# Two tiles' input products as 2 by 2 blocks with seven block products, in a pooled-attention and gated feed-forward kernel

## Chip, cores and metric

The kernel runs on one core of a Trainium2 chip. The metric is the device time of one execution in microseconds; the median of several runs is compared. A profile of one execution, taken by the hardware profiler, shows what each engine did.

## The reference

```python
# B, H, S, D = 8, 8, 576, 64; d_model 512, d_ff 1536; all float32
k_p = k.reshape(B, H, Sp, 8, D).mean(axis=3)          # Sp = 72
v_p = v.reshape(B, H, Sp, 8, D).mean(axis=3)
scores = scale * np.matmul(q, k_p.transpose(0, 1, 3, 2))
scores = scores - np.max(scores, axis=-1, keepdims=True)
attn = np.exp(scores)
attn = attn / (np.sum(attn, axis=-1, keepdims=True) + 1e-09)
x = np.matmul(attn, v_p)        # then to [4608 tokens, 512]
out = ((x @ w_a) * (x @ w_b)) @ w_out
```

Attention over pooled keys and values gives 4608 rows of 512; a feed-forward part multiplies two projections of them and projects back.

## The kernel before

The 4608 tokens are cut into nine tiles of 512. For each tile and each of twelve feature blocks of 128 (`f`), `ffn_in` computes the two input products (names `a` and `b`) into the PSUM tiles `psa` and `psb`, `gated` multiplies them, and `ffn_out` adds the output product into the four PSUM tiles `acc`. Float32 precision is kept by splitting every operand into a high part of a shorter type and a low part, the difference: each product is three matmuls, high by high, high by low, low by high (lines 618 to 620 and 640 to 642). So a feature block of one tile costs 24 matmuls of 512 columns for the inputs (4 slices of the 512 model dimensions, 3 matmuls, 2 names) and 12 for the output. The high part is a copy on ScalarE (lines 264, 588), the low part a subtraction on VectorE or POOL (`low_part`, line 185).

The weights lie whole in SBUF (`raw`). They arrive as 64-bit words and are turned into float32 by ScalarE and VectorE while tiles 0 and 1 are computed (`convert_weights`). For every tile each weight block is split anew (`split_weight`), on POOL after tile 0.

The attention is computed in chunks of up to 128 queries of one batch (`chunk`): queries split, scores into `psc`, softmax, transposes of the probabilities into `ptr`, and, for blocks of chunks of up to 256 queries in tiles 0 and 1 and up to 384 later, the value products `po`, which are split into the tile's `xh` and `xl`. PSUM tiles of the attention share the tag `att` with two buffers. Keys and values of a batch are pooled by `load_keys` and `load_values`.

The order of all this is written by a small scheduler, `Chains`: every piece of side work is a generator that yields a number of steps; each call of `chains.step()` in the matmul loops (one for six large matmuls) lets those that are due write their next instructions, and one group of small matmuls (`yield PE`). The list `order` holds the large products (tiles 0 and 1 interleaved, because the weights come slowly there; then tile by tile, the output product one block behind), and `plan` the step at which each split, chunk and load begins. All DMAs are issued by SyncE (SP), in the order in which they were written. Every engine works through its own instructions in order.

Of the kernel before, what the change touches and what calls it, by code (L numbers as in the profile page):

```python
# [9 lines left out]
F32 = mybir.dt.float32  # L10
# [39 lines left out]
SLOTS = 6  # L50
TILE_SLOTS = SLOTS * NF

BLOCK, BLOCK_LATER = 256, 384
# [13 lines left out]
IN, OUT = 4, 2  # L67
# [4 lines left out]
CHUNK = 33  # L72
SECOND_GAP, SECOND_START = 1, 14
KEYS_AHEAD, VALUES_AFTER = 18, 14
# [49 lines left out]
def attn_moe_kernel(ctx: ExitStack, tc: tile.TileContext, q, k, v, vr, wa, wb, wo, out):  # L124
# [16 lines left out]
    raw = {name: const.tile([P, NF, 512], F32, name=f"w{name}_raw") for name in ("a", "b", "o")}  # L141
# [8 lines left out]
    work = sb.tile([P, 2 * NK * BLOCK_LATER], I32, tag="work", name="words", bufs=1)  # L150
# [21 lines left out]
    while start < len(flat):  # L172
        stop = start
        while stop < len(flat) and flat[stop][0] == flat[start][0] and tile_of[stop] == tile_of[start]:
            stop += 1
        blocks += cut(list(range(start, stop)), BLOCK if tile_of[start] < 2 else BLOCK_LATER)[1]
# [3 lines left out]
    early_p = {}  # L180
    upcoming = {name: [] for name in ("a", "b", "o", "h")}
    held = dict.fromkeys(upcoming, 0)
# [5 lines left out]
    early_q = raw["a"][:, NF - early:, :].rearrange("p c (g s) -> p c g s", g=NK)  # L188
    early_k = raw["b"].rearrange("p f c -> p (f c)")[:, NF * 512 - NK * S:].rearrange("p (g s) -> p g s", g=NK)
    early_v = raw["o"][:, NF - NK:, :]  # L190
    early_vr = raw["o"][:, NF - NK - NG:NF - NK, :]
# [17 lines left out]
    def convert_weights(name, j, first):  # L209
# [11 lines left out]
        for f in range(NF):  # L221
            words = area[name].rearrange("p (c w) -> p c w", w=2)
            hi, lo = words[:, :, 1], words[:, :, 0]
            w = raw[name][:, f, :]
# [15 lines left out]
            yield 2  # L240

# [16 lines left out]
    def split_weight(name, x):  # L258
        f = x % NF
        yield from wait(("weight", name, f))  # L260
        yield from room(name, x)
        hi = sb.tile([P, 512], F32R, tag=f"jh{name}", name=f"jh{name}_{x}")
        lo = sb.tile([P, 512], F32R, tag=f"jl{name}", name=f"jl{name}_{x}")
        nc.scalar.copy(hi, raw[name][:, f, :])  # L264
        yield 1
        low_part(nc.vector if x < NF and name != "o" else nc.gpsimd, lo, raw[name][:, f, :], hi)
        parts[name, x] = hi, lo

    def load_keys(b):
        kd = kdiag[b % 2]  # L270
        kp = tmp(f"kp_{b}")[:, :NK * SP].rearrange("p (g s) -> p g s", g=NK)
        for g0 in range(0, NK, 2):
# [3 lines left out]
            else:  # L276
# [5 lines left out]
                yield 4  # L282
# [25 lines left out]
            mark("keys", b, g0)  # L308

    def load_values(b):  # L310
        vd = vdiag[b % 2]
        vrem = sb.tile([P, NG, 2, 2, D], F32R, tag="vrem", name=f"vrem_{b}")
        yield from wait(("keys", b, 2), ("values", b - 1))
        vp = sb.tile([P, NK + NG, D], F32, tag="vp", name=f"vp_{b}", bufs=1)
        for x0 in range(0, NK + NG, 2):
            if b == 0:
                vraw = [early_v[:, x, :] if x < NK else early_vr[:, x - NK, :] for x in (x0, x0 + 1)]
            else:
# [8 lines left out]
                yield 3  # L327
# [12 lines left out]
            yield 1  # L340
        for e in range(2):
            r = slice(e * KM, e * KM + KM)
            nc.scalar.mul(vd[r, :, 0, r], vp[r, :NK], 1.0 / POOL)
# [36 lines left out]
    def chunk(i):  # L380
# [5 lines left out]
        else:  # L386
            qraw = tmp(f"qraw_{i}").rearrange("p (g s) -> p g s", g=NK)
            if soon:
                yield from wait(("scores", i - 2))
            load_raw_queries(i, qraw)  # L390
            yield 3 if soon else 5
# [5 lines left out]
        low_part(nc.gpsimd if first else nc.vector, ql[:, :, :n], qraw[:, :, :n], qh[:, :, :n])  # L397
# [17 lines left out]
        if i < SUMMED:  # L415
            for g0 in range(0, NK, 2):
                yield from wait(("keys", b, g0))
                yield PE
                if first:
                    pt = ps.tile([P, 512], F32, tag="acc", name=f"psc_{i}_{g0}", bufs=4)  # L420
                else:
                    pt = ps.tile([P, 512], F32, tag="att", name=f"psc_{i}_{g0}", bufs=2)
                for j in range(2):
                    g = g0 + j
                    for x, (qq, w) in enumerate(((qh, 0), (qh, 1), (ql, 0))):
                        nc.tensor.matmul(
                            pt[:n, j * hk:(j + 1) * hk],
                            qq[:, g, :n],
                            kd[:, g, w].rearrange("p e s -> p (e s)"),
                            start=(x == 0),  # L430
                            stop=(x == 2),
                        )
                less_max(slice(2 * g0, 2 * g0 + 4), pt[:n, :2 * hk].rearrange("p (h s) -> p h s", h=4))
        else:
            for g in range(NK):
                yield from wait(("keys", b, g - g % 2))
                if g % 2 == 0:
                    yield PE
                pt = ps.tile([P, 512], F32, tag="att", name=f"psc_{i}_{g}", bufs=2)
                nc.tensor.matmul(  # L440
                    pt[:n, :2 * hk], qh[:, g, :n], kd[:, g].rearrange("p w e s -> p (w e s)"), start=True, stop=False
                )
                nc.tensor.matmul(  # L443
                    pt[:n, :hk], ql[:, g, :n], kd[:, g, 0].rearrange("p e s -> p (e s)"), start=False, stop=True
                )
                nc.vector.tensor_reduce(
                    out=s[:n, 2 * g:2 * g + 2, :].rearrange("p h s -> p (h s)"),
                    in_=pt[:n, :2 * hk].rearrange("p (w c) -> p c w", w=2),
                    axis=AX.X,
                    op=ALU.add,  # L450
                )
                if g % 2 and g < NK - 1:
                    yield 1
            yield 1
            less_max(slice(0, H), s[:n])
# [36 lines left out]
        def turn(x):  # L492
            rows = P if x < 2 else NR
            num = NK if x < 2 else NG
            if x not in turned[j]:
                if j == 0:

                    if x != 1:
# [303 lines left out]
```

## Time and profile before

| | us |
|---|---|
| median of 3 runs | 1068.54 |
| lowest, highest | 1067.54, 1070.07 |
| profiled execution, first to last instruction (its span; the profile shows nothing outside it) | 1069.4 |
| tiles 0 and 1, from the first large matmul to tile 2 (50.24 to 297.91) | 247.67 |
| tile 4, tile 5, tile 6, tile 7 | 113.0, 110.4, 114.3, 108.6 |

The mean granted TensorE clock of the execution is 0.992 of full speed. The DMA queues moved 63.26 MB, 59 GB/s in the mean. In the profile's tables, PE is TensorE, PEld its weight loads, DVE is VectorE, ACT ScalarE, POOL GpSimd, SPq SyncE's queue. A matmul's length in the timeline is that of its pipeline; how fast matmuls follow each other is read from their starts. "idle before, releaser" is the time for which an engine had nothing to do just before a group's instructions, and what ended it.

### The profile page before, as it was taken

To read this page: it belongs to the slowest core of one execution; us is meant where nothing else is said; L and a number is where in the kernel's file an instruction comes from. 1 tells how busy PE (TensorE), PEld (TensorE's weight loads), DVE (VectorE), ACT (ScalarE), POOL (GpSimd) and SP (SyncE) were. 2 spreads that over 40 slices of the span, in tenths; PEclk is the share of its full clock that TensorE was granted. 3 is DMA by queue.
4 is the path that set the end of the run, shared out by engine and by line. 5 is a ranking of instruction groups with operands and counts; after the bars stand their busy time and mean duration, and the time that the engine had idled before them with its cause. 6 is when DMAs were issued, how large, how long until landed. Compare 5 with 4: busy or idle time off the path is not lost.

```text
span 1069.4 us, 13397 instructions
## 1 busy us (share of the span) xinstructions
PE 1029.1 (96%) x4964; PEld 855.9 (80%) x4964; DVE 622.7 (58%) x941; ACT 515.1 (48%) x1037; POOL 520.8 (49%) x427
## 2 busy tenths in 40 slices
PE   4678999999999999999999999999999999999998
PEld 4556788888878888888887888888887888888886
DVE  7997967955674455644676456654668444423222
ACT  3756745554553445544544454444545444443332
POOL 6331200255474555555556555555556455554443
PEclk9988999999999999999999999999999999999999
DMA  6343445330330003100320002100220010001001
GB/s 218 117 137 119 138 125 193 116 131 2 105 111 1 1 23 110 46 1 1 97 91 1 1 28 84 45 1 1 94 71 14 1 60 1 1 1 40 1 1 40
DMA packets 31889, 63.26 MB, mean 59 GB/s; under 512 B 7344, under 2 KB 7344, under 8 KB 31824
## 3 DMA queue, kind: packets, MB, share of 16 engines
q1 hardware_dynamic: 31824, 62.40, 18.3%
q8 instruction: 39, 0.64, 0.2%
q14 instruction: 26, 0.21, 0.1%
HBM read 51.12 MB, written 11.27 MB: 58 GB/s over the span
## 4 chain that ended last, share of the span: by engine, by line
PE 88%; DVE 7%; ACT 3%; issue 1%; DMA 0%; POOL 0%; SPq 0%; DVEq 0%; ACTq 0%; POOLq 0%
PE acc L640 9%; PE psa L618 9%; PE acc L642 9%; PE psb L618 9%; PE acc L641 9%; PE psa L620 9%; PE psa L619 9%; PE psb L620 9%; PE psb L619 9%; PE ptr L521 2%; PE psc L440 2%; PE po L558 1%; PE po L559 1%; PE psc L443 1%; PE po L557 1%; PE po L556 1%
## 5 line engine op out<-in xcount | busy, mean ns | idle before, releaser
L185 POOL TENSOR_TENSOR jlo<-wo_raw,jho 128x512 fp32r<-128x512 f32 x108 | 141.2, 1308 | 423.5 <-ACT jho L264 423.4
L625 ACT COPY h<-psa 128x512 f32<-128x512 f32 x108 | 63.5, 588 | 255.6 <-PE psa L620 234.0
L575 DVE TENSOR_TENSOR h<-psb,h 128x512 f32<-128x512 f32 x108 | 74.1, 686 | 191.9 <-PE psb L620 186.2
L640 PE MATMUL acc<-jho,hh 128*128 128x512 f32 x432 | 173.6, 402 | 0.0
L618 PE MATMUL psa<-xh,jha 128*128 128x512 f32 x432 | 173.2, 401 | 0.4 <-DVE xl L185 0.4
L618 PE MATMUL psb<-xh,jhb 128*128 128x512 f32 x432 | 171.2, 396 | 0.0
L619 PE MATMUL psa<-xl,jha 128*128 128x512 f32 x432 | 169.9, 393 | 0.1
L620 PE MATMUL psa<-xh,jla 128*128 128x512 f32 x432 | 169.9, 393 | 0.0
L642 PE MATMUL acc<-jho,hl 128*128 128x512 f32 x432 | 169.4, 392 | 0.0
L641 PE MATMUL acc<-jlo,hh 128*128 128x512 f32 x432 | 169.2, 392 | 0.0
L620 PE MATMUL psb<-xh,jlb 128*128 128x512 f32 x432 | 168.4, 390 | 0.0
L619 PE MATMUL psb<-xl,jhb 128*128 128x512 f32 x432 | 168.2, 389 | 0.0
L185 POOL TENSOR_TENSOR jla<-wa_raw,jha 128x512 fp32r<-128x512 f32 x89 | 134.4, 1510 | 8.5 <-ACT jha L264 8.5
L185 DVE TENSOR_TENSOR hl<-h,hh 128x512 fp32r<-128x512 f32 x101 | 106.6, 1055 | 28.8 <-ACT hh L588 28.1
L185 POOL TENSOR_TENSOR jlb<-wb_raw,jhb 128x512 fp32r<-128x512 f32 x89 | 118.0, 1326 | 0.1
L620 PEld LDWEIGHTS psa<-xh,jla 128*128 128x128 f32 x432 | 82.0, 190 | 17.7
L642 PEld LDWEIGHTS acc<-jho,hl 128*128 128x128 f32 x432 | 81.5, 189 | 17.6
L620 PEld LDWEIGHTS psb<-xh,jlb 128*128 128x128 f32 x432 | 81.1, 188 | 17.2
L618 PEld LDWEIGHTS psa<-xh,jha 128*128 128x128 f32 x432 | 81.9, 190 | 16.0 <-DVE xl L185 0.7
L619 PEld LDWEIGHTS psa<-xl,jha 128*128 128x128 f32 x432 | 82.1, 190 | 15.7 <-DVE xl L185 0.5
L185 DVE TENSOR_TENSOR ql<-qraw,qh 128x512 fp32r<-128x512 f32 (+1 forms) x36 | 41.6, 1157 | 90.0 <-ACT qh L395 90.0
L618 PEld LDWEIGHTS psb<-xh,jhb 128*128 128x128 f32 x432 | 81.1, 188 | 15.4 <-DVE h L575 0.2
(102 smaller groups left out, 1737.6 us busy)
## 6 DMA issues: line engine op xcount, KB each, us to landing
out<-y SPq DMA_DIRECT2D x36, 256.0 KB, 2.0
kraw<-in_k SPq DMA_DIRECT2D x28, 288.0 KB, 3.2
vraw<-in_v SPq DMA_DIRECT2D x28, 256.0 KB, 3.0
qraw<-in_q SPq DMA_DIRECT2D x28, 256.0 KB, 3.6
words<-in_wa SPq DMA_DIRECT2D x12, 512.0 KB, 3.6
words<-in_wb SPq DMA_DIRECT2D x12, 512.0 KB, 3.7
words<-in_wo SPq DMA_DIRECT2D x12, 512.0 KB, 3.6
vraw<-in_vr SPq DMA_DIRECT2D x14, 192.0 KB, 2.5
```

Of the source, the lines that this page charges most:

```text
L185: eng.tensor_tensor(out=lo, in0=src, in1=hi.bitcast(F32), op=ALU.subtract)
L440: nc.tensor.matmul(pt[:n, :2 * hk], qh[:, g, :n], kd[:, g].rearrange("p w e s -> p (w e s)"), start=True, stop=False)
L443: nc.tensor.matmul(pt[:n, :hk], ql[:, g, :n], kd[:, g, 0].rearrange("p e s -> p (e s)"), start=False, stop=True)
L521: nc.tensor.transpose(ptr[:rows, g, :n], src, ident[:n, :n])
L575: nc.vector.tensor_tensor(out=h, in0=pt, in1=h, op=ALU.mult)
L618: nc.tensor.matmul(pt, wh[:, c], xh[:, kk], start=(kk == 0), stop=False)
L619: nc.tensor.matmul(pt, wh[:, c], xl[:, kk], start=False, stop=False)
L620: nc.tensor.matmul(pt, wl[:, c], xh[:, kk], start=False, stop=(kk == NK - 1))
L625: nc.scalar.copy(h, pt)
L640: nc.tensor.matmul(acc[c], hh[:, cs], wh, start=first, stop=False)
L641: nc.tensor.matmul(acc[c], hh[:, cs], wl, start=False, stop=False)
L642: nc.tensor.matmul(acc[c], hl[:, cs], wh, start=False, stop=last)
```

## The change

Tiles 0 and 1 stay as they were, but for the attention around them. Tile 2 is computed alone, all input products first, then all output products. Tiles 3 to 8 are taken in pairs. For a pair and a feature block, the two tiles are the rows, the two halves of the model dimensions the inner index and the names a and b the columns of a 2 by 2 block product. Its eight block products are replaced by seven, of weight sums and differences (`T1` to `T4`, `A0`, `A1`, `B1`) with sums of the tiles' halves (`X00`, `X01`, `X11`, `S1` to `S4`), and additions of the results. `both` does this: 7 x 2 x 3 = 42 large matmuls, five additions on VectorE that read PSUM, two operations on POOL and two copies on ScalarE. Three PSUM banks hold the products: `psa`, `psb`, and one of the two of the tag `att`. The first tile's output product runs in the gaps of the next blocks; the second's gated values go to DRAM (`keep_later`) and come back for twelve output blocks in a row after the pair.

- The weight sums are made once, on POOL, ScalarE and VectorE, while tiles 1 and 2 run (`sums_of_weights`), and written to DRAM with the split parts of `a` and `b` (`jd`); the converted output weights go there too (`od`). In the pairs SBUF holds four buffers of 2 MB, and `loads` streams one feature block's fourteen parts and its output weights into each.
- The attention's results of tiles 2 to 8 go to DRAM unsplit (`xd`). `whole_x` loads tile 2's; `sums_of_x` loads a pair's and makes and splits the seven sums, at the output products that stand before the pair.
- The attention of tiles 2 to 4 is planned beside tiles 0 to 2, that of tiles 5 and 6 beside the first pair, of 7 and 8 beside the second. From the tenth chunk on, scores are six matmuls of 144 columns for half a chunk and copied by ScalarE, where two of 288 and two of 144 were added up by VectorE. Value blocks are at most 256 queries. The low parts of later queries move from VectorE to POOL.

The core of the diff (the new `sums_of_weights`, `loads` and `sums_of_x` are told above):

```diff
-BLOCK, BLOCK_LATER = 256, 384
+BLOCK = 256
-IN, OUT = 4, 2
+IN, OUT, BOTH, REST = 4, 2, 9, 3
+PAIRS = [(3, 4), (5, 6), (7, 8)]
...
-        low_part(nc.vector if x < NF and name != "o" else nc.gpsimd, lo, raw[name][:, f, :], hi)
+        shared = name == "o" and (t in (1, 2) or t > 3 and t % 2 == 0 and f % 2)
+        low_part(nc.vector if x < NF and name != "o" or shared else nc.gpsimd, lo, src, hi)
...
+                to = big(f"j{at}_{f}")
+                nc.sync.dma_start(to[:, :2 * JW], jd[f].rearrange("p h c s -> p (h c s)"))
+                nc.sync.dma_start(to[:, 2 * JW:], od[:, f])
...
+            if i < SUMMED:
+                less_max(slice(2 * g0, 2 * g0 + 4), src)
+            else:
+                nc.scalar.copy(s[:n, 2 * g0:2 * g0 + 4], src)
...
+    def both(p, f):
+        t0, t1 = PAIRS[p]
+        need(lambda: (p, f) in stream and ("combos", p, S4) in done)
+        w, xs = stream[p, f], combos[p]
+        u, v, r = banks if f % 2 == 0 else (banks[2], banks[1], banks[0])
...
+        product(u, A0, X00)
+        nc.scalar.copy(first, u)
+        product(v, T2, S2)
+        add(nc.vector, first, v, first)
+        rest(0)
+        product(u, A1, X01, start=False)
+        product(r, T3, S3)
+        add(nc.vector, third, r, first)
+        chains.step()
+        rest(1)
+        product(v, T1, S1)
+        nc.scalar.copy(fifth, v)
+        product(r, T4, X11)
+        add(nc.gpsimd, fifth, fifth, third)
+        add(nc.vector, fourth, r, third)
+        add(nc.gpsimd, fifth, fifth, fourth, ALU.mult)
+        rest(2)
+        product(v, B1, S4, start=False)
+        add(nc.vector, first, v, first)
+        add(nc.vector, first, u, first, ALU.mult)
...
-    for t in range(2, NTILE):
-        for f in range(NF):
-            order.append(("in", t, f))
-            if f:
-                order.append(("out", t, f - 1, f == 1, False))
+    order += [("in", 2, f) for f in range(NF)] + [("out", 2, f, f == 0, f == NF - 1) for f in range(NF)]
+    for p, (t0, t1) in enumerate(PAIRS):
+        order += [("both", p, f) for f in range(NF)] + [("rest", p)]
+        order += [("out", t1, f, f == 0, f == NF - 1) for f in range(NF)]
```

Two places show how the order of instructions changes. First TensorE, before, inside a feature block of tile 3 (`psc` are scores, `psa` an input product, each row one matmul):

```order
L440 MATMUL psc_0_4313<-kdiag_75,qh_4236 128x288
L443 MATMUL psc_0_4313<-kdiag_75,ql_4237 128x144
L440 MATMUL psc_1_4317<-kdiag_75,qh_4236 128x288
L443 MATMUL psc_1_4317<-kdiag_75,ql_4237 128x144
L618 MATMUL psa_5_4301<-xh_3125,jha_4246 128x512
L619 MATMUL psa_5_4301<-xl_3126,jha_4246 128x512
L620 MATMUL psa_5_4301<-xh_3125,jla_4247 128x512
```

And TensorE after, inside the third block of the first pair (`bank` are the seven products, six matmuls each, `acc` output products of earlier blocks, a quarter at a time):

```order
L820 MATMUL bank_psa<-x_1_4059,j_2_4371 128x512 x6
L820 MATMUL bank_att<-x_5_4060,j_2_4371 128x512 x6
L885 MATMUL acc_3_4688<-jo_later,hh_4493 128x512
L886 MATMUL acc_3_4688<-jo_later,hh_4493 128x512
L887 MATMUL acc_3_4688<-jo_later,hl_4494 128x512
L618 MATMUL psc_0_4695<-kdiag_78,qh_4616 64x144 x2
L618 MATMUL psc_0_4695<-kdiag_78,ql_4617 64x144
L618 MATMUL psc_0_4695<-kdiag_78,qh_4616 64x144 x2
L618 MATMUL psc_0_4695<-kdiag_78,ql_4617 64x144
L820 MATMUL bank_psb<-x_3_4061,j_2_4371 128x512 x6
```

The quarters of an output product and the attention's groups now stand between products of six, and half a chunk's scores are six matmuls of 144 columns.

Second VectorE, before, at the ninth to eleventh feature block of tile 2 (`h` is the gate, `hl` its low part, `kp` and `kdiag` the keys of a later batch, `ql` and `xl` low parts of queries and attention results):

```order
L185 TENSOR_TENSOR hl_3574<-h_3529,hh_3573 128x512
L575 TENSOR_TENSOR h_3606<-psb_9_3608,h_3606 128x512
L185 TENSOR_TENSOR hl_3655<-h_3606,hh_3654 128x512
L284 TENSOR_REDUCE kp_3626<-kraw_0_3627 128x72
L284 TENSOR_REDUCE kp_3626<-kraw_1_3628 128x72
L185 TENSOR_TENSOR ql_3696<-qraw_3624,qh_3695 128x512
L575 TENSOR_TENSOR h_3689<-psb_10_3691,h_3689 128x512
```

And VectorE after, at four output blocks of tile 2 (`back` are gated values from DRAM, `jo_later` the output weights' parts, `temp` and `x` the sums for the first pair and their low parts):

```order
L216 TENSOR_TENSOR hl_4096<-back_4037,hh_4095 128x512
L216 TENSOR_TENSOR jo_later<-wo_0_3500,jo_later 128x512
L402 TENSOR_TENSOR temp_4127<-x_3987 128x512 x2
L216 TENSOR_TENSOR hl_4116<-back_4069,hh_4115 128x512
L216 TENSOR_TENSOR jo_later<-wo_0_3500,jo_later 128x512
L402 TENSOR_TENSOR temp_4128<-temp_4127,x_3987 128x512 x2
L216 TENSOR_TENSOR hl_4144<-back_4099,hh_4143 128x512
L216 TENSOR_TENSOR jo_later<-wo_0_3500,jo_later 128x512
L472 TENSOR_REDUCE kp_3925<-kraw_2_4085 128x72
L216 TENSOR_TENSOR hl_4169<-back_4119,hh_4168 128x512
L216 TENSOR_TENSOR x_4_4058<-temp_4128,x_4_4058 128x512 x2
L216 TENSOR_TENSOR jo_later<-wo_0_3500,jo_later 128x512
```

Where a block of 36 large matmuls had a gate and a low part, an output block of 12 now has a low part of the gate, one of the weights, and two operations of the pair's sums between them. The row that follows is the second reduction of `kp`.

More of the change, by code (lines that the diff above doesn't have):

```diff
@@ L175, in attn_moe_kernel @@
             stop += 1
-        blocks += cut(list(range(start, stop)), BLOCK if tile_of[start] < 2 else BLOCK_LATER)[1]
+        blocks += cut(list(range(start, stop)), BLOCK)[1]
         start = stop
@@ L258, in split_weight @@
     def split_weight(name, x):
-        f = x % NF
-        yield from wait(("weight", name, f))
-        yield from room(name, x)
-        hi = sb.tile([P, 512], F32R, tag=f"jh{name}", name=f"jh{name}_{x}")
-        lo = sb.tile([P, 512], F32R, tag=f"jl{name}", name=f"jl{name}_{x}")
-        nc.scalar.copy(hi, raw[name][:, f, :])
+        t, f = divmod(x, NF)
+        if t < 3 and (name != "o" or t < 2):
+            yield from wait(("weight", name, f))
+            src = raw(name, f)
+        else:
+            while name == "o" and x not in wo_later:
+                yield 1
+            src = wo_later[x]
@@ L269, in load_keys, with claim, of_batch @@
+    busy = set()
+    def claim(what):
+        while what in busy:
+            yield 1
+        busy.add(what)
+    def of_batch(b):
+        return [i for i in range(len(flat)) if flat[i][0] == b]
     def load_keys(b):
+        yield from wait(*(("scores", i) for i in of_batch(b - 2)))
+        if b:
+            yield from claim("kv")
         kd = kdiag[b % 2]
@@ L387, in chunk @@
             qraw = tmp(f"qraw_{i}").rearrange("p (g s) -> p g s", g=NK)
-            if soon:
-                yield from wait(("scores", i - 2))
+            yield from wait(("scores", i - 2))
             load_raw_queries(i, qraw)
-            yield 3 if soon else 5
+            yield 3 if soon else 8
         yield from wait(("scores", i - 2))
@@ L413, in less_max @@
             )
[L415 to L453, printed above, removed]
@@ new lines, in chunk @@
+        for g0 in range(0, NK, 2):
+            yield from wait(("keys", b, g0))
+            yield PE
+            if first:
+                pt = ps.tile([P, 512], F32, tag="acc", name=f"psc_{i}_{g0}", bufs=4)
+            else:
+                pt = ps.tile([P, 512], F32, tag="att", name=f"psc_{i}_{g0}", bufs=2)
+            for j in range(2):
+                g = g0 + j
+                for x, (qq, w) in enumerate(((qh, 0), (qh, 1), (ql, 0))):
+                    nc.tensor.matmul(
+                        pt[:n, j * hk:(j + 1) * hk],
+                        qq[:, g, :n],
+                        kd[:, g, w].rearrange("p e s -> p (e s)"),
+                        start=(x == 0),
+                        stop=(x == 2),
+                    )
+            src = pt[:n, :2 * hk].rearrange("p (h s) -> p h s", h=4)
+            if i < SUMMED:
+                less_max(slice(2 * g0, 2 * g0 + 4), src)
+            else:
+                nc.scalar.copy(s[:n, 2 * g0:2 * g0 + 4], src)
+                yield 1
@@ L628, in attn_moe_kernel, with keep_later, rest_of, ffn_out @@
+    def keep_later(x, h):
+        later[x] = dram.tile([P, NT], F32, name=f"later_{x}")
+        nc.sync.dma_start(later[x], h)
+        yield 1
+    waiting = []
+    def rest_of(p):
+        while waiting:
+            if len(waiting) % 2 == 0:
+                chains.step()
+            waiting.pop(0)()
     acc = {}
-    def ffn_out(t, f, first, last):
+    def ffn_out(t, f, first, last, cs=None):
         x = t * NF + f
@@ L633, in ffn_out @@
         (wh, wl), (hh, hl) = parts["o", x], parts["h", x]
-        for c in range(NT // P):
-            if c % 2 == 0:
+        for c in cs or range(NT // P):
+            if c % 2 == 0 and not cs:
                 chains.step()
```

337 lines of the change are left out of this document (271 added, 66 removed).

## The prediction

> **What bounds the kernel now.** I read the page first, then a table of windows cut at the stages, then the order of time on TensorE.
>
> ```profile
> span 1069.4 us, 13397 instructions
> PE 1029.1 (96%) x4964; PEld 855.9 (80%) x4964; DVE 622.7 (58%) x941; ACT 515.1 (48%) x1037; POOL 520.8 (49%) x427
> PE   4678999999999999999999999999999999999998
> PE 88%; DVE 7%; ACT 3%; issue 1%; DMA 0%; POOL 0%; SPq 0%; DVEq 0%; ACTq 0%; POOLq 0%
> ```
>
> TensorE is busy for 96% of the span and carries 88% of the chain that ends last; VectorE's 7% lies at the start. The stages show it (windows; the columns are named in the first line):
>
> ```profile
> core 0: us, PE busy (x) PEld busy (x) DVE busy (x) ACT busy (x) POOL busy (x), PEclk, DMA share, GB/s
> 0.00:50.24 50.24, 27.69 (x145) 25.27 (x145) 42.43 (x81) 26.08 (x58) 24.57 (x34) 1.00 0.54 175
> 50.24:99.66 49.42, 39.80 (x183) 30.94 (x183) 42.01 (x71) 30.67 (x65) 12.81 (x12) 0.83 0.39 120
> 99.66:123.42 23.76, 20.63 (x107) 16.07 (x105) 22.25 (x38) 15.76 (x33) 8.67 (x7) 1.00 0.44 133
> 123.42:209.15 85.73, 85.45 (x386) 70.36 (x386) 67.52 (x110) 46.17 (x86) 8.10 (x6) 1.00 0.48 152
> 209.15:229.22 20.07, 20.07 (x108) 17.05 (x106) 13.14 (x21) 9.41 (x20) 10.47 (x8) 1.00 0.13 47
> 229.22:250.18 20.96, 20.96 (x103) 17.51 (x102) 13.06 (x21) 10.45 (x22) 10.80 (x9) 1.00 0.39 129
> 250.18:297.91 47.73, 47.73 (x233) 40.16 (x232) 28.19 (x43) 24.29 (x51) 26.43 (x22) 1.00 0.20 63
> 297.91:408.50 110.59, 110.15 (x544) 91.39 (x542) 63.00 (x98) 53.77 (x114) 63.46 (x51) 1.00 0.13 39
> 855.79:964.36 108.57, 108.57 (x529) 90.97 (x528) 45.34 (x62) 49.10 (x96) 60.47 (x48) 1.00 0.05 15
> 964.36:1065.20 100.84, 100.80 (x445) 83.17 (x443) 25.46 (x28) 34.53 (x62) 43.01 (x34) 1.00 0.04 13
> 1065.20:1069.40 4.20, 0.00 (x0) 0.00 (x0) 0.69 (x1) 0.00 (x0) 0.00 (x0) 0.96 0.54 199
> ```
>
> Up to 50.24 stands the start, up to 297.91 tiles 0 and 1, then one tile takes some 110 us. From tile 2 on TensorE is never idle, and VectorE is at 57% (63.00 of 110.59). Only at 50 to 123 us is VectorE the bound: busy 85 to 94%, with TensorE waiting for 12.7 us. So a matmul saved after 123 us is time saved, as long as nothing else becomes late. The pace of a large matmul is read from two starts, 42 matmuls apart:
>
> ```profile
> 1000.40 0.39 PE L618 MATMUL psb<-xh,jhb 128*128 128x512 f32 x1
> ...
> 1009.92 0.39 PE L618 MATMUL psb<-xh,jhb 128*128 128x512 f32 x1
> ```
>
> 9.52 us for 42: 0.2267 us each (the 0.39 is a pipelined length). Of 512 columns there are 9 x 12 x 36 = 3888, 881 us.
>
> **The change: matmuls.** Before, one feature block of two tiles costs 48 large matmuls for the input products; now seven products of 6 cost 42. Over 3 pairs and 12 blocks that is 216 fewer: **-49.0 us**. All else on TensorE grows. The scores of the later 31 chunks now come as six matmuls of 144 columns for half a chunk, where two of 288 and two of 144 stood. Both shapes are in the trace:
>
> ```profile
> 94.21 0.40 PE L620 MATMUL psb<-xh,jlb 128*128 128x512 f32 x1
> ...
> 95.08 0.43 PE L640 MATMUL acc<-jho,hh 128*128 128x512 f32 x1
> ...
> 219.36 0.40 PE L620 MATMUL psb<-xh,jlb 128*128 128x512 f32 x1
> ...
> 220.04 0.44 PE L618 MATMUL psb<-xh,jhb 128*128 128x512 f32 x1
> ```
>
> Between the first two starts lie six small matmuls, between the last two four: 0.87 - 0.23 = 0.64 us against 0.68 - 0.23 = 0.45. 62 halves by 0.19 make **+12**. Value products come in blocks of at most 256 columns where 384 were allowed: 64 more matmuls, the columns unchanged. That lies between 0 and 64 x 0.107 (0.64 / 6) = 7; with the transposes of the remainder, which now stand in groups of their own, I take **+5**. TensorE's work falls by **32 us**.
>
> **The change: the other engines.** POOL loses most of the weight parts, the pairs' weights being loaded ready made. VectorE gains in three places; its prices:
>
> ```profile
> L575 DVE TENSOR_TENSOR h<-psb,h 128x512 f32<-128x512 f32 x108 | 74.1, 686 | 191.9 <-PE psb L620 186.2
> L185 DVE TENSOR_TENSOR hl<-h,hh 128x512 fp32r<-128x512 f32 x101 | 106.6, 1055 | 28.8 <-ACT hh L588 28.1
> L185 DVE TENSOR_TENSOR hl<-h,hh x101: 639/1076/1790, 73.3 to 1061.2; 128x512 fp32r<-128x512 f32 x101
> L284 DVE TENSOR_REDUCE kp<-kraw 128x72 f32<-128x576 f32 x28 | 20.3, 738 | 0.1
> L300 DVE SCALAR_TENSOR_TENSOR kdiag<-kp,kdiag 64x144 fp32r<-64x144 f32 x32 | 18.3, 573 | 2.2 <-ACT kdiag L295 1.6
> L522 ACT CAST p<-ptr 128x512 fp32r<-128x512 f32 x60 | 35.1, 587 | 31.4 <-PE ptr L521 31.4
> ```
>
> *Inside a pair* each block adds five VectorE additions that read PSUM (0.69, 3.4 us), where two gates (1.4) stood, and two POOL operations. A block is 54 large matmuls, 12.2 us, and about 2 us of attention, so VectorE's 5 us and its share of attention hide. The closest bank is free again 9 large matmuls (2.0 us) after its product, against 0.69 for the addition that reads it. I cost these at nothing; uncovered, an addition costs its 0.69. The attention of tiles 5 to 8 has one PSUM bank instead of two: a group waits for the copy of the one before (0.59 on ScalarE, in its turn). Some 57 groups a pair for two pairs: between 0 and 114 x 0.59 = 67 us. Mostly six large matmuls (1.4 us) lie between two groups, at the least three (0.7 us), which cover the copy unless ScalarE, at half load, is behind: **+3**. At a pair's end the output products of the last block wait for addition, gate and split (0.69 + 0.69 + 0.6 + 0.7, about 2.7 us) behind 9 matmuls (2.0 us): +0.7 each, **+2**.
>
> *Tiles 0 and 1.* The attention of tiles 2 to 4 is brought forward, and the weight sums are made here: 350 VectorE instructions for 301. The six rows from 50.24 to 297.91 add up to 186 us for 304 records, 0.61 each; 49 more are 30 us at that, 52 at 1.055. I take 40: 226 us of VectorE in some 273 us (247.7, and 20 us of attention that stood later). That is the share at which the stretch from 123 to 209 ran almost without a wait (67.52 of 85.73, 79%), a little above it: waits **+5**, bounds 0 and 40.
>
> *Tile 2 alone.* Its output products stand behind one another, 12 matmuls (2.72 us) a block. The order above shows four blocks (10.9 us): 14 VectorE operations with two SBUF operands and two reductions, 14 x 0.64 + 1.5 = 10.5 to 14 x 1.055 + 1.5 = 16.3 us. All twelve (34 us with one chunk's scores) hold 32 such operations and 17 others, at 0.61 each: 31 to 44 us. VectorE is late by 0 to 10 us, and the pair's first products wait behind it: **+6**. The same place after tile 4 has half the weight parts, after tile 6 no keys: **+3** and **+2**.
>
> *DMA.* A pair's block streams 2.1 MB in 12 to 14 us.
>
> ```profile
> 150.00:200.00 50.00, 50.00 (x224) 41.39 (x223) 39.42 (x64) 27.07 (x50) 5.19 (x4) 1.00 0.57 181
> back<-later SPq DMA_DIRECT2D x7, 256.0 KB, 5.0
> ```
>
> 181 GB/s took 0.57 of the queues with TensorE busy throughout, so I expect no loss at 150 to 175 GB/s, four buffers deep. During tile 2's input products (288 large and 92 small matmuls, 75 us) 24 MB pass: 10 writes of weight sums (5.2), 23 of weight parts (8.9), 11 of gated blocks (2.9), 3.1 of output weights and 4 of the rest. That is 320 GB/s, and 181 / 0.57 is 318: full. SP issues all of it in order, 461 transfers for 200, and a write that waits for POOL holds back what is behind it; a pair's blocks are asked for some three blocks (36 us) ahead, so this is hidden there. Behind tile 2's writes stand the loads of stored products (5.0 us from issue to landing, asked for 8.2 us ahead). Between 0 and 45 us (at 200 GB/s); most writes are needed only a stage later, so **+1**. The Trainium skill, page "DMA: Bandwidth & Descriptors", section Specifications, puts the HBM limit of one core at about 358 GB/s; by that the 24 MB would take 67 us and the term would be 0, and no run here shows such a rate.
>
> Sum: -32 + 3 + 2 + 5 + 6 + 3 + 2 + 1 = **-10 us** against the profiled 1069.4, which lies 0.9 above the median of the runs. Forecast: 1068.5 - 10 = **1059 us**.
>
> **Rivals.** *All cover holds:* the waits vanish as in tile 7 (108.57 of 108.57 busy) and only the matmuls count: 1068.5 - 32, some **1037**. Against it speaks VectorE at tile 2's output products, which only the shortest price ever seen lets through in time.
>
> *VectorE becomes the bound (slower).* From 123 to 209 us POOL was nearly idle (8.10 of 85.73). Now POOL makes weight sums and low parts of the queries there. The split of h shows what a busy POOL may do to a VectorE operation with two SBUF operands: 0.64 to 1.79 for one shape. Some 60 of these in tiles 0 and 1 and 90 at the three places above, each dearer by 0.25 than priced, make 37 us, of which two thirds stand on the path: +24, **1083**. It decides once VectorE needs over 16.5 us for a block of tile 0 with one of tile 1 and an output block (60 matmuls, 13.6 us, and 3 us of attention).
>
> *The streams are late (slower):* tile 2's writes at 200 GB/s instead of 318 take 121 us for 75; +30 is left after slack, **1089**.
>
> *The clock falls at the new boundaries (no change).*
>
> ```profile
> 82.79 0.69 PE L521 MATMUL ptr<-ident,pr 64*128 64x64 f32 x4 [2.44 <-ACT p L522]
> 80.00:85.00 5.00, 2.56 (x9) 1.86 (x9) 4.86 (x10) 4.20 (x9) 0.00 (x0) 0.50 0.35 105
> 85.00:90.00 5.00, 5.00 (x18) 3.46 (x17) 3.54 (x6) 0.44 (x3) 0.00 (x0) 0.56 0.52 135
> ```
>
> After a wait of 2.44 us in a half-idle stretch the granted clock was 0.50, then 0.56 for 5 us: 2.2 us lost. Should it fall so at five of the six places where a pair begins or ends, +11: **1070**. The Trainium skill ("TensorE: Matmul & The Clock Gate", Part 1: The HAM clock gate) asks for an idle window of about 3.4 us; by that my waits of 1 to 3 us would not do it. The row shows less, though with another wait just before.
>
> **Chances.** Forecast (1050 to 1066) 0.45, cover holds (1034 to 1050) 0.20, clock or an even balance (within 0.2%, about what a measurement of this kernel can tell from no change: 1066.4 to 1070.7) 0.10, VectorE 0.17, streams 0.08. Faster 0.65, same 0.10, slower 0.25. The range takes in the cover and most of VectorE's case: 1036 to 1084.
>
> **What would show it.** Per pair, 504 matmuls of the seven products at 0.227; a block near 14.2 us with attention and 12.3 in the last pair; a row of waits at tile 2's output products naming VectorE; the stage of tiles 0 and 1 at about 273 us. It is wrong if that stage exceeds 290 us, if products wait for DMA, or if TensorE's pace leaves 0.227 while the streams run.

## The result and the profile after

The changed kernel takes 1119.91 us (median of 5 runs, 1114.91 to 1121.37), the kernel before 1070.07 beside it: a ratio of 1.0465 (95% interval 1.0442 to 1.0488). The forecast was 1059, the range up to 1084: wrong in its sign and outside its range. The profiled execution was the shortest of the five (1114.91). Lines of the page of the changed kernel:

```profile
span 1113.1 us, 14035 instructions
PE 1032.7 (93%) x4936; PEld 836.7 (75%) x4936; DVE 665.8 (60%) x963; ACT 491.8 (44%) x986; POOL 488.8 (44%) x412
PE 71%; DVE 17%; ACT 4%; issue 3%; POOL 3%; DMA 2%; SPq 0%; DVEq 0%; POOLq 0%; ACTq 0%
j<-jd SPq DMA_DIRECT2D x36, 1792.0 KB, 7.4
```

TensorE's share of the chain that ends last fell from 88 to 71%, VectorE's rose from 7 to 17%. The streams (`j<-jd`) are not on it to speak of. Tiles 0 and 1 as one window (same columns as before):

```profile
50.59:350.83 300.24, 271.53 (x1321) 220.02 (x1321) 245.59 (x349) 176.76 (x361) 127.94 (x106) 0.93 0.48 157
```

And the windows of their last two stretches, and of most stages after them:

```profile
263.43:297.88 34.45, 30.29 (x139) 24.15 (x138) 33.68 (x36) 18.58 (x38) 25.32 (x20) 0.86 0.54 184
297.88:350.83 52.95, 51.97 (x258) 42.62 (x258) 38.93 (x47) 30.14 (x58) 31.19 (x26) 0.96 0.43 146
350.83:427.64 76.81, 76.13 (x382) 63.32 (x382) 35.02 (x47) 40.07 (x78) 53.26 (x45) 1.00 0.88 313
427.64:474.50 46.86, 37.48 (x157) 27.82 (x156) 37.13 (x50) 21.43 (x36) 16.98 (x12) 1.00 0.62 232
474.50:652.21 177.71, 173.39 (x880) 140.94 (x879) 86.59 (x139) 67.60 (x149) 77.31 (x69) 1.00 0.57 206
652.21:705.34 53.13, 47.08 (x209) 36.31 (x208) 39.81 (x46) 27.06 (x46) 30.43 (x20) 0.97 0.59 213
876.41:926.01 49.60, 45.53 (x198) 35.17 (x196) 33.99 (x37) 25.43 (x41) 27.39 (x18) 0.97 0.56 200
926.01:1068.92 142.91, 142.91 (x624) 116.96 (x622) 47.40 (x70) 26.12 (x48) 43.52 (x34) 1.00 0.54 199
```

Tiles 0 and 1 take 300.2 us, where 273 were forecast. The stages of output products after tiles 2, 4 and 6 take 46.9, 53.1 and 49.6, where their matmuls alone are some 34, 42 and 41 (an estimate: 144, 169 and 170 large ones at 0.2267 us and 13, 38 and 26 small ones at 0.1). The products of tile 2 (76.8) stream at 313 GB/s with TensorE busy for 76.13, and the last pair's (142.91) never wait. So the loss lies where VectorE is busy for 69 to 98% of the stretch *and* POOL works beside it. One place of the first slow stretch (timeline; start, length, engine, what):

```profile
271.61 0.69 DVE L753 TENSOR_TENSOR h<-psb,h 128x512 f32<-128x512 f32 x1 [0.38 <-PE psb L799]
...
273.45 1.47 POOL L216 TENSOR_TENSOR pr<-s,pr 64x512 fp32r<-64x512 f32 x1
273.81 6.93 DVE L216 TENSOR_TENSOR sums<-sums 128x512 fp32r<-128x512 f32 x1
...
274.89 0.31 POOL L216 TENSOR_TENSOR rem<-s,rem 64x64 fp32r<-64x64 f32 x1
275.17 1.28 POOL L216 TENSOR_TENSOR xl<-xl,xh 128x512 fp32r<-128x512 f32 x1
...
276.42 1.27 POOL L216 TENSOR_TENSOR jab<-wab,jab 128x512 fp32r<-128x512 f32 x1
...
277.66 1.28 POOL L216 TENSOR_TENSOR xl<-xl,xh 128x512 fp32r<-128x512 f32 x1
...
278.91 1.27 POOL L326 TENSOR_TENSOR sums<-wab 128x512 f32<-128x512 f32 x1
...
280.26 1.07 POOL L328 TENSOR_TENSOR sums<-wab,sums 128x256 f32<-128x256 f32 x1
```

A VectorE subtraction with two SBUF operands takes 6.93 us. It starts while POOL is at `pr`, waits through the rest of that and five more POOL operations, and ends at 280.74, 0.56 us after POOL's first gap opens (280.18 to 280.26). VectorE's queue stands meanwhile. POOL's next operation, begun at 280.26, then takes 1.07 us, where operations of its line take 0.72 to 0.74 with VectorE idle: it waits in its turn.

Taken over all 221 such subtractions of 512 columns in this trace (the split of a value into its high and low part, line 216, none reading PSUM), the two prices lie apart: the 142 that began with no POOL operation under way took 0.69 us at most; the 79 that began during one took 1.54 in the median. The kernel before has the same two: 69 at 0.70 at most, and 91 at 1.36 in the median. The Trainium skill ("SBUF — State Buffer", SBUF: two separate sides) has the two engines share one pair of ports as an exclusive lock, the later one blocked until the first is done. The trace agrees that one is blocked, not slowed in proportion; but here it was blocked through a row of POOL operations, not one.

TensorE's clock fell with the waits: the mean granted clock is 0.975 over 1113.1 us, against 0.992 over 1069.4 before. That is up to 28 us lost to pace, against up to 9 (an estimate: 1 less the clock, times the span; an upper bound, as TensorE stood for part of that time).

### The profile page after: what moved, and what is told of

The parts are those of the page before. It is cut to its first block, busy times and chain, and to the rows that moved or that the text cites. A ratio compares the mean times of both kernels' runs of the same rounds, so it can differ in the third digit from the quotient of the medians.

```text
span 1113.1 us, 14035 instructions
## 1 busy us (share of the span) xinstructions
PE 1032.7 (93%) x4936; PEld 836.7 (75%) x4936; DVE 665.8 (60%) x963; ACT 491.8 (44%) x986; POOL 488.8 (44%) x412
## 4 chain that ended last, share of the span: by engine, by line
PE 71%; DVE 17%; ACT 4%; issue 3%; POOL 3%; DMA 2%; SPq 0%; DVEq 0%; POOLq 0%; ACTq 0%
PE bank_psb L820 13%; PE bank_att L820 9%; PE bank_psa L820 8%; PE acc L885 7%; PE acc L886 7%; PE acc L887 7%; PE psc L618 4%; PE psa L797 2%; PE ptr L691 2%; PE psb L797 2%; PE psa L799 2%; DVE hl L216 2%; PE psa L798 2%; PE psb L798 2%; PE psb L799 2%
## 5 line engine op out<-in xcount | busy, mean ns | idle before, releaser
L826 POOL TENSOR_TENSOR temp<-temp,temp 128x512 f32<-128x512 f32 x72 | 93.1, 1294 | 218.4 <-ACT temp L843 201.2
L820 PE MATMUL bank_psb<-x,j 128*128 128x512 f32 x648 | 168.4, 395 | 0.0
L886 PE MATMUL acc<-jo_later,hh 128*128 128x512 f32 x336 | 135.8, 404 | 14.9 <-DVE jo_later L216 13.0
L885 PE MATMUL acc<-jo_later,hh 128*128 128x512 f32 x336 | 136.8, 407 | 2.7 <-ACT jo_later L305 2.7
L820 PEld LDWEIGHTS bank_psb<-x,j 128*128 128x128 f32 x648 | 118.9, 188 | 24.4
L887 PE MATMUL acc<-jo_later,hl 128*128 128x512 f32 x336 | 134.5, 400 | 1.9 <-DVE hl L216 1.9
L826 DVE TENSOR_TENSOR temp<-bank_psb,temp 128x512 f32<-128x512 f32 x72 | 49.7, 690 | 114.4 <-PE bank_psb L820 107.4
L820 PE MATMUL bank_psa<-x,j 128*128 128x512 f32 x432 | 112.1, 394 | 1.0 <-ACT temp L833 1.0
L820 PE MATMUL bank_att<-x,j 128*128 128x512 f32 x432 | 111.8, 394 | 0.0
L820 PEld LDWEIGHTS bank_psa<-x,j 128*128 128x128 f32 x432 | 79.6, 188 | 18.0 <-ACT temp L833 1.3
L820 PEld LDWEIGHTS bank_att<-x,j 128*128 128x128 f32 x432 | 79.5, 188 | 16.3
L886 PEld LDWEIGHTS acc<-jo_later,hh 128*128 128x128 f32 x336 | 64.4, 192 | 35.4 <-DVE jo_later L216 19.9
L885 PEld LDWEIGHTS acc<-jo_later,hh 128*128 128x128 f32 x336 | 63.7, 190 | 16.6 <-ACT jo_later L305 3.1
```

Source lines behind the costliest of these rows:

```text
L820: nc.tensor.matmul(bank, w[:, wh, wc, k], xs[xc][:, xh, k], start=start and not k and not n, stop=k == HALF - 1 and n == 2, skip_group_che ...
L826: eng.tensor_tensor(out=out, in0=a, in1=b, op=op)
L885: nc.tensor.matmul(acc[c], hh[:, ct], wh, start=first, stop=False)
L886: nc.tensor.matmul(acc[c], hh[:, ct], wl, start=False, stop=False)
L887: nc.tensor.matmul(acc[c], hl[:, ct], wh, start=False, stop=last)
```

## Experiments

Stages in us of the profiled executions, beside the median of the runs. They are cut at the first large matmul of a stage; a pair ends within its last product (the expectations cut out 4 and out 6 some 1.2 us later). "Left out" marks the kernels without a part of the arithmetic; the kernel before was at 1069.8 to 1070.1 beside all of them.

| | median | tiles 0, 1 | tile 2 in | out 2 | pair 0 | out 4 | out 6 |
|---|---|---|---|---|---|---|---|
| changed kernel | 1119.9 | 300.2 | 76.8 | 46.9 | 177.7 | 53.1 | 49.6 |
| e1_x_none (left out) | 1103.6 | 300.4 | 76.8 | 44.5 | 178.9 | 48.5 | 45.0 |
| e2_w_none (left out) | 1106.6 | 291.0 | 75.8 | 50.8 | 178.0 | 54.8 | 49.8 |
| e3_x_dve | 1106.2 | 300.5 | 76.8 | 44.1 | 179.0 | 48.1 | 47.0 |
| e4_x_pool | 1133.3 | 300.2 | 76.9 | 49.5 | 177.6 | 59.2 | 58.0 |
| e5_all_low | 1088.4 | 285.2 | 76.2 | 44.6 | 176.3 | 47.6 | 44.1 |
| e6_no_pool | 1093.5 | 286.6 | 75.9 | 44.6 | 177.2 | 47.8 | 44.2 |
| e9_pool_twice | 1141.0 | 311.3 | 88.0 | 47.5 | 177.7 | 53.1 | 49.7 |
| e10_best | 1158.7 | 294.8 | 76.8 | 48.3 | 199.6 | 59.3 | 47.1 |
| e11_best_late | 1152.5 | 276.1 | 90.1 | 51.4 | 194.0 | 59.8 | 45.3 |
| e13_low_first | 1086.8 | 287.3 | 76.1 | 45.5 | 176.4 | 47.6 | 44.1 |
| e14_low_late | 1099.6 | 266.4 | 83.2 | 80.9 | 168.8 | 47.7 | 44.1 |
| e15_low_late_x | 1095.0 | 268.4 | 83.2 | 75.8 | 168.0 | 47.8 | 43.9 |

### Which work, and on which engine

The theory: VectorE stands still while POOL works. The rival: VectorE simply has too much work. First the sums of x were left out of the arithmetic (a part of the edit; the two stored sums became copies too).

```diff
-            for k in range(HALF):
-                low_part(eng, lo[:, k], src[:, k], hi[:, k])
+            nc.scalar.copy(lo, src)
...
```

> Left out: the sums and differences of the gated-input blocks and their low parts (the two stored sums and the low parts are plain ScalarE copies instead), so VectorE and POOL have nothing to do for the combinations of x at the three output stages. Theory A (these 18 VectorE and 15 POOL operations make VectorE the bound there): the three output stages, 46.9, 51.9 and 48.4 us in the changed kernel, fall to 37 to 41 each, and the time falls from 1120 to about 1090. Rival B (the output weights' split or the chain of addition, gate and split of h is what waits, whatever stands beside it): the stages keep 45 us or more, time 1113 or more. Both: tiles 0 and 1 stay at 300 us, tile 2's input products at 77.

16 us less, not 30: the stages fell by 2 to 5, to 44.5, 48.5 and 45.0, between what theory A and rival B expect. The sums of x are a part of the loss. (The expectations count 18 operations on VectorE and 15 on POOL at a stage; the trace has 36 and 30 for the three stages, so 12 and 10.) The run is a poor one for the rest, since the copies put in their place made ScalarE busy for 35.4 of out 4's 48.5 us.

In the next run the weight sums' arithmetic is left out.

> Left out: the sums of the weight blocks and their split (raw weights are written to DRAM in their place, in the same number and size of transfers). Theory A (in tiles 0 and 1 VectorE beside POOL is what makes 300 us out of the forecast 273, and the weight sums bring 24 VectorE and 36 POOL operations there): the stage of tiles 0 and 1 falls by at least 10 us, from 300 to 290 or less, time 1110 or less. Rival B (it is the attention brought forward, with its small matmuls, softmax and value copies, whatever the weight sums do): the stage falls by less than 4 us, time 1116 or more.

9 us less in tiles 0 and 1, just short of the 10 of theory A, more than twice the 4 of rival B; VectorE was busy for 218.16 there instead of 245.59, 27 us less with 15 records fewer. This run takes away POOL's work and VectorE's together, so it does not tell the theory from the rival of amount.

Then the sums of x moved whole to one engine or the other, with nothing left out.

```diff
-        yield from parted(X00, x00, nc.gpsimd)
+        yield from parted(X00, x00, nc.vector)
...
-        s3 = summed(x10, nc.gpsimd, x00, x10, ALU.subtract)
+        s3 = summed(x10, nc.vector, x00, x10, ALU.subtract)
...
```

> All 33 operations of the sums and low parts of x on VectorE, none on POOL, nothing left out. If VectorE is slowed by POOL beside it (the operations then take 0.65 to 0.75 us instead of 1.2 to 1.8): VectorE needs 33 x 0.7 = 23 us in place of 18 x 1.5 = 27, the three output stages get shorter by 3 to 6 us each, time about 1107. If it is the amount of VectorE work at a price that POOL does not set (1.055 each): 15 operations more, 16 us a stage, less what waited for POOL: each stage longer by 5 to 12 us, time 1135 to 1155.

> All 33 operations of the sums and low parts of x on POOL, none on VectorE, nothing left out. If VectorE's own amount is the bound in the output stages: 18 operations go away from it, the output products keep pace (stages 38 to 42 us), but POOL needs 33 x 1.3 to 1.75 = 43 to 58 us, so the pair's first products wait up to 10 us for the last sums: time between 1100 and 1130. If what binds is the two engines side by side (each slowing the other), POOL slows the splits of h as long as it runs: the stages keep 47 us or more, time 1125 to 1145.

On VectorE alone, with 10 operations a stage more for it, the time falls by 13.7 us, nearly as much as by leaving the sums out (16.3). On POOL alone it rises by 13.4. More work for VectorE and less time: the rival of amount is out for this part. Out 4 with all on VectorE shows both prices within 5 us (timeline of that run, VectorE and POOL):

```profile
672.25 0.69 DVE L216 TENSOR_TENSOR jo_later<-wo,jo_later 128x512 fp32r<-128x512 f32 x1
...
675.00 1.50 POOL L216 TENSOR_TENSOR jo_later<-wo,jo_later 128x512 fp32r<-128x512 f32 x1 [4.30 <-ACT jo_later L305]
675.26 1.79 DVE L216 TENSOR_TENSOR hl<-back,hh 128x512 fp32r<-128x512 f32 x1
```

0.69 with POOL idle, 1.79 as soon as a POOL operation (started 0.26 earlier) runs. With all on POOL its queue is what the output weights wait for (waits of TensorE in out 4; engine, line, what it waited for, us in total, times, longest):

```profile
PE acc L886 <- POOL jo_later L216: 8.4, 3, 4.2
PE acc L886 <- DVE jo_later L216: 1.4, 2, 0.8
```

### The suspected cost taken away and doubled

All low parts, all sums of x and all weight sums on VectorE, then POOL without any arithmetic after the start; and the other way round, each POOL difference of the weight sums done twice in the changed kernel. A part of the first edit:

```diff
     def low_part(eng, lo, src, hi):
-        eng.tensor_tensor(out=lo, in0=src, in1=hi.bitcast(F32), op=ALU.subtract)
+        nc.vector.tensor_tensor(out=lo, in0=src, in1=hi.bitcast(F32), op=ALU.subtract)
...
```

> All sums of x as in the run with them on VectorE, and every low part and all weight sums on VectorE too; POOL keeps the two additions a block of the pairs, the division of the probabilities and a few value sums. Nothing left out. Theory A (a VectorE operation with two SBUF operands waits while POOL works: 6.93 us for one beside eight POOL operations in a row): VectorE's operations take 0.7, the stage of tiles 0 and 1 falls from 300 to 288 or less and the three output stages to 40 to 45, time 1085 to 1098. Rival B (VectorE has too much work, whoever stands beside it): some 60 operations more in tiles 0 and 1, 40 us, so 246 + 40 = 286 us of VectorE and a stage of 305 or more; time 1115 or more.

> As the kernel with all low parts on VectorE, and the rest of POOL's arithmetic too (additions of the pairs, division of the probabilities, value sums): POOL does nothing after the start. Theory A: all VectorE operations at their shortest (0.68 to 0.69 for 512 columns), stage of tiles 0 and 1 within 5 us of the run before this one, time within 6 us of it. Rival B: 30 divisions and 72 additions more, each 0.7 to 0.9: longer by 15 us or more than the run before this one.

> The changed kernel with each of the 36 POOL differences of the weight sums done twice (the second writes the same again): 39 us of POOL more in tiles 0 and 1, nothing more on VectorE, TensorE or the queues. Theory A (VectorE waits while POOL works): VectorE's operations there get longer, the stage of tiles 0 and 1 goes from 300 to 308 to 325, time 1128 to 1145. Rival B (VectorE's own amount of work): POOL, 128 + 39 of 300 us, is not the bound; stage and time within 4 us of the changed kernel.

All three times are as the theory had it: 1088.4 (with out 4 at 47.6, over the 45 expected), 1093.5, and 1141.0 when POOL alone got more to do (11 us more in tiles 0 and 1, and 11 in tile 2's input products, into which the weight sums now ran). In the first, VectorE does 91 operations more in tiles 0 and 1 than in the changed kernel and is busy for 4 us less (same columns as before; 245.59 for 349 there):

```profile
52.60:337.78 285.18, 260.58 (x1322) 211.87 (x1321) 241.29 (x440) 176.50 (x361) 18.60 (x15) 0.97 0.51 165
```

That rules the amount of VectorE's work out for these 15 us. The doubled POOL work is the weaker test: VectorE's busy time in tiles 0 and 1 rose by only 6 us (251.29), and TensorE now waited 4.3 us there and 8.3 in tile 2's input products for results of POOL itself (none and 0.7 in the changed kernel). So about half of those 22 us is POOL's own queue. The moves to VectorE, too, take POOL's longer operations (1.29 us for 0.69) out of the chains; how their 31.5 us divide between that and the stalls was not separated, and by the granted clock (0.987 over 1084.6 us, so up to 14 us lost to pace where it was up to 28) some 14 of them may be TensorE's clock.

The dearest groups before and after the move (groups by form; the mean in ns of one), first the changed kernel:

```profile
L216 DVE TENSOR_TENSOR hl<-back,hh 128x512 fp32r<-128x512 f32 x55 | 50.1, 910 | 55.0 <-ACT hh L766 54.7
L216 DVE TENSOR_TENSOR sums<-sums 128x512 fp32r<-128x512 f32 x24 | 33.5, 1404 | 14.9 <-ACT sums L331 14.8
L216 DVE TENSOR_TENSOR hl<-h,hh 128x512 fp32r<-128x512 f32 x17 | 18.7, 1102 | 1.9 <-ACT hh L766 1.9
```

and with all low parts on VectorE (groups, and a line of its page):

```profile
L216 DVE TENSOR_TENSOR hl<-back,hh 128x512 fp32r<-128x512 f32 x55 | 37.8, 687 | 41.6 <-ACT hh L766 41.3
L216 DVE TENSOR_TENSOR sums<-sums 128x512 fp32r<-128x512 f32 x24 | 17.4, 725 | 2.4 <-ACT sums L331 2.4
L216 DVE TENSOR_TENSOR hl<-h,hh 128x512 fp32r<-128x512 f32 x17 | 11.6, 683 | 0.4 <-ACT hh L766 0.4
```

```profile
PE 1016.9 (94%) x4936; PEld 829.0 (76%) x4936; DVE 718.5 (66%) x1246; ACT 491.9 (45%) x986; POOL 162.1 (15%) x129
```

283 more VectorE instructions cost it 53 us more, 0.19 each. By their own groups in this run (0.68 to 0.73 for 512 columns, less for the narrow ones) they take some 171: so some 118 of VectorE's 666 us in the changed kernel had been standing still (an estimate).

The kernel before was treated alike:

> The kernel before with all its low parts on VectorE. Theory A: its VectorE operations get their 0.69 back, but from tile 2 on TensorE waited for nothing, so there is little to win: 1058 to 1070, by waits before 300 us only. Rival B: VectorE gets 36 low parts more a tile, 63 + 25 = 88 of 110 us, and becomes late: 1080 or more.

```profile
PE 1029.8 (96%) x4964; PEld 855.8 (80%) x4964; DVE 727.7 (68%) x1311; ACT 512.2 (48%) x1037; POOL 62.1 (6%) x57
```

Here 370 instructions, 236 us by their groups, cost VectorE 105: it too had been held up, by some 131 us. But the time rose a little (1.0065, interval 1.0047 to 1.0083; half of it a first large matmul at 53.18 us for 50.24). From tile 2 on VectorE stood off the path there, so taking the same lockout away gained nothing.

### Terms of the sum

The new scores, and the smaller value blocks, each alone in the kernel before:

> The kernel before with the new scores alone (six matmuls of 144 columns and a ScalarE copy for half a chunk in place of four matmuls and VectorE reductions). The prediction's term: 62 halves by 0.19 us = +12, time 1080 to 1083. Rival: six small matmuls cost hardly more than four where weight loads or waits already stood, +4 or less, time 1074 or less.

> The kernel before with value blocks of at most 256 columns where 384 were allowed, and nothing else. The prediction's term: +5 (between 0 and 7), time 1073 to 1077. Rival: the smaller blocks cost nothing or their waits cost more than 8 us.

+7.8 us (ratio 1.0078, 1.0061 to 1.0094) where the sum had 12 and the rival 4 or less, and +3.3 (1.0035, 1.0020 to 1.0049) where it had 5. Both mis-sized by a third in the same direction: with the 49.0 counted they would make TensorE's gain 38, not 32.

The traces of the changed kernels don't show that gain. An estimate of TensorE's work is the mean spacing of starts (without those after a wait or at half clock) times the number. Before, 3888 large matmuls came at 0.2306 us and 1076 small ones at 0.112, 1017 us in all; in the changed kernel 3672 came at 0.2357 and 1264 at 0.105, 998; in e5_all_low the sum is 997. So the work fell by some 19 us. By the same measure the new scores alone are +7 and the smaller blocks +3, as their times say. The other half of the 38 went because the next start came 0.005 us later after a large matmul: 0.2346 to 0.2357 us in seven traces with the change, 0.2306 to 0.2308 in the kernel before and its three variants. It is so with POOL idle too (0.2354), so the stalls are not the cause; what is was not tested.

### What is left of the gap, and can a version beat both?

> All low parts and sums on VectorE as in the run that gave 1088.4, but those of the first batch's chunks left on POOL (the start was 2 us longer without), and before's scores (four matmuls, VectorE reduction). Nothing left out. If the scores cost the 7.8 us that the kernel before lost by them: 1088.4 - 2 - 8 = 1078 (1075 to 1082). If VectorE, now with 128 operations fewer on POOL, has no room for 122 reductions more: 1086 or more.

> The run with before's scores, and the attention of tiles 2 to 4 spread from tile 1's block 0 on and not from its block 5 (some 60 us later), into tile 2's input products, where VectorE is at half load. If VectorE's load at 130 to 225 us is what is left of the loss there: 5 to 12 us less than the run before this one, 1066 to 1073. If it only moves the work onto the streams and waits of tile 2: within 3 us of it, or more.

A plain miss for both: 1158.7, some 70 us more than without before's scores, and with later attention 1152.5. Waits of TensorE in the first pair of e10_best:

```profile
PE psc L633 <- DVE s L639: 18.7, 16, 3.5
```

In the second pair the same wait is 19.7 us. In the pairs the attention has one PSUM bank. Before's scores fill it four times for a chunk and have VectorE empty it each time, the new ones twice, with ScalarE. So the new scores, dearer by 7.8 us where two banks were free, suit the one bank better; the two waits named are 38 of the 70 us, and the rest was not followed up.

The three last runs keep the new scores. The first leaves the first batch's low parts on POOL, the second moves the attention later, the third delays a load (cuts of the second's and the third's edit):

```diff
...
-        spans = {t: (2, place["in", 1, LAG], place["out", 2, 0] - EARLIER) for t in range(2, PAIRS[1][0])}
+        spans = {t: (2, place["in", 1, 0], place["out", 2, 0] - EARLIER) for t in range(2, PAIRS[1][0])}
...
+                    if r and not at:
+                        yield 6
                     nc.sync.dma_start(to[:, r], xd[t])
...
```

> The kernel with all low parts and sums on VectorE (1088.4), but the low parts of the first batch's chunks left on POOL. Its start was 52.6 us in place of 50.6. If the 2 us come from these: 1086 to 1087. If POOL's work there makes VectorE wait as it does later: 1088 or more.

> As the run before this one, with the attention of tiles 2 to 4 spread from tile 1's block 0 on and not from its block 5. Theory: what is left of the loss in tiles 0 and 1 (285 us for 240 of matmuls) is VectorE's amount of work while the weights are rebuilt there, so less attention in that stretch saves 4 to 8 us of the sum of tiles 0, 1 and 2: 1079 to 1083. Rival: what is left there are the chains of single waits that stood there before the change too (20 us), and attention only moves: within 3 us of the run before this one.

> As the run before this one, with the load of the second stored x tile of pair 0 given six steps later. In the run with all low parts on VectorE the queues are full when tile 2's output products begin (share 1.01, 391 GB/s), a stored product is late and TensorE waits 3.67 us. If that transfer is what it stood behind: tile 2's output stage falls from 44.6 to 40 to 42, time 2 to 4 us less. If the sums of x, which need it, then end too late: the same or up to 5 us more.

The first batch's low parts are worth at most 1.6 us (1086.8, ratio 1.0156, 1.0138 to 1.0174, against 1088.4); the first large matmul is back at 50.6 us from 52.6. Later attention takes 21 us out of tiles 0 and 1, of which some 12 are matmuls that moved and 9 lost time; the theory of VectorE's amount of work there holds that far. But the time, 1099.6, is a miss for both expectations: the attention overran the end of tile 2, and the output stage nearly doubled (waits of TensorE in it):

```profile
PE ptr L691 <- ACT pr L653: 12.7, 1, 12.7
PE psc L618 <- ACT xo L740: 11.2, 2, 10.8
```

The delayed load makes that stage 5 us shorter, and the wait for `xo` falls from 11.2 to 3.7 us, so the transfer had been in the way there; but the stage is 75.8 us, not the 40 to 42 expected. Whether it is in the way in e13's schedule wasn't tried. No version beat the kernel before. The best, e13_low_first, is 1.6% slower than it and 33 us faster than the change as made.

## Why the prediction was wrong

- **The step that failed** is the price of VectorE's operations: 0.61 us a record in tiles 0 and 1, taken from six rows in which POOL was busy for 77 of 248 us, and for tile 2's output products between 0.64 and 1.055. It took the price as VectorE's own. It is one of POOL's schedule: 245.59 us for 349 records, 0.70 each, where 226 were forecast, since an operation that met POOL took 1.5 to 1.8 as a rule and 6.9 once. Waits of "+5, bounds 0 and 40" became 32 (300.2 for the 268 that its sum has without them), inside its bounds but far from the value taken, and the output stages' +6, +3 and +2 became some +13, +11 and +9.
- **The rival that came true** is "VectorE becomes the bound". It had the mechanism and the engine beside it, and was 37 us too low (1083): 0.25 dearer for 150 operations is 37 us of VectorE, and the runs show some 118 over the whole kernel. It got 0.17 all the same. The prediction did read the wide spread of the split of h (0.64 to 1.79) as what a busy POOL may do, but put 0.25 on a mean. Read against POOL's rows of the same moments, the spread would have shown two prices (0.70 at most, or 1.36 in the median).
- **A second step that failed** is TensorE's own work: -32 in the sum, some -19 by the spacing of starts. The prediction kept the large matmul at 0.2267 us and put a slower pace at nothing; the 0.005 us more of the 3672 large matmuls make some 19 us.
- **Shown by the runs:** of the 61 us between forecast and result, 31.5 go when POOL's low parts and sums go (1119.9 to 1088.4). The other 29 are in part VectorE's amount of work in tiles 0 and 1 (9 us, by moving attention) and a late stored product at the start of tile 2's output stage (one wait of 3.67 us in e5_all_low, below). That leaves some 16 us, and 6 more if the gain had been 38; the slower pace is some 19 of these 22. The few that remain, and the reason for the slower pace, stay open.
  The window and, from the timeline, TensorE's wait of that place in e5_all_low, where the queues are full. The wait is put down to the split of the output weights; ScalarE had stood before it until a stored product (`back`) came:

```profile
413.94:424.00 10.06, 6.25 (x26) 4.52 (x24) 2.71 (x5) 1.82 (x3) 0.00 (x0) 1.00 1.01 391
```

```profile
422.18 0.62 ACT L766 CAST hh<-back 128x512 fp32r<-128x512 f32 x1 [8.77 <-DMA back<-later]
423.37 0.49 PE L885 MATMUL acc<-jo_later,hh 128*128 128x512 f32 x1 [3.67 <-ACT jo_later L305]
```

- **The clock** fell at waits shorter than thought. In out 4 of the changed kernel (timeline of TensorE, and the window of that place, granted clock 0.57):

```profile
697.60 0.50 PE L886 MATMUL acc<-jo_later,hh 128*128 128x512 f32 x1 [1.78 <-POOL jo_later L216]
...
698.18 0.63 PE L885 MATMUL acc<-jo_later,hh 128*128 128x512 f32 x1
698.61 0.63 PE L886 MATMUL acc<-jo_later,hh 128*128 128x512 f32 x1
...
701.80 0.40 PE L885 MATMUL acc<-jo_later,hh 128*128 128x512 f32 x1
697.60:701.20 3.60, 3.60 (x10) 2.81 (x11) 3.57 (x4) 0.54 (x1) 2.92 (x2) 0.57 0.00 0
```

  After a wait of 1.78 us matmuls follow each other at 0.43 us, half pace, for 3 us. A wait of 1.21 us some 5 us earlier (at 692.77) was not followed by this. In all, pace cost up to 28 us, against up to 9 before (worked out above). This rival had +11 at boundaries, and it came as an addition to longer waits rather than as a case of its own. The rule cited for it (the Trainium skill, "TensorE: Matmul & The Clock Gate", Part 1: The HAM clock gate) would not have let 1.78 us do this; the trace decides.
- **Right:** the pairs (177.7, 171.1 and 142.9 us; VectorE's additions and the bank turn hide but for some 5 us of waits, where 3 were forecast), the streams (36 loads of 1.8 MB with no wait for them), tile 2's input products at 313 GB/s for the 320 foreseen. The rate that the Trainium skill gives as the limit ("DMA: Bandwidth & Descriptors", Specifications, about 358 GB/s) was passed: 391 GB/s for 10 us in e5_all_low.
- **Of its own tests**, "wrong if that stage exceeds 290 us" is the one that caught it. The one on TensorE's pace points at the second step, but the streams are not its reason: two large matmuls in a row start 0.233 us apart already in tiles 0 and 1, before the first stream (0.229 there in the kernel before).

## What to carry to other kernels

Price an operation with two SBUF operands on VectorE by what POOL does at that moment, not by a group's mean: min and maximum in the trace are two states, and a kernel in which VectorE is hidden shows the dear state at no cost until a change puts VectorE on the path. Where it is on the path, moving such work *from* POOL *to* VectorE can shorten both. And when large matmuls are saved, look first at the stages between them: here some 19 us of TensorE's work were bought with sums whose place was already the tightest one.

## What the runs showed of the hardware

- A VectorE subtraction of two SBUF operands, 0.69 us at most when none of POOL's is under way at its start, waited through six POOL operations in a row (6.93 us), while POOL's of 512 columns on 128 partitions took 1.27 to 1.28, their usual 1.29; a gap of 0.08 us in POOL's row let it through.
- It is not only operations with two operands: the 36 of `TENSOR_SCALAR` in the weights' conversion (line 260, one SBUF operand) took 0.43 us at most with POOL idle (e6_no_pool) and up to 1.50 in the changed kernel. The reductions of the scores (`m<-s`, one SBUF operand) took 0.74 to 0.75 either way.
- VectorE's additions that read PSUM took 0.69 us beside POOL as well, as the group in the pairs shows, where POOL was busy for 77 of 178 us:

```profile
L826 DVE TENSOR_TENSOR temp<-bank_psb,temp 128x512 f32<-128x512 f32 x72 | 49.7, 690 | 114.4 <-PE bank_psb L820 107.4 <-ACT temp L833 7.0
```

- A wait of 1.78 us was enough for 3 us of matmuls at half pace (granted clock 0.57 from 697.60 to 701.20).
